# Column halves for the last row group, and row-by-row output stores in the last four blocks

## The chip, the cores and the metric

The kernel runs on one core of a Trainium2 chip. The metric is the device time of one execution in microseconds (us); a profiled execution also has a span, from the program's first recorded instruction to its last, about 1.8 us shorter. TensorE (the matmul engine) is called PE, its weight loads PEld, VectorE DVE, ScalarE ACT, GpSimd POOL and SyncE SP in the profile; a q after the name (SPq) marks work of the engine's sequencer, such as issuing a DMA.

## The reference, cut to what matters

```python
sig = 1.0 / (1.0 + np.exp(-f_logit))
f = lower_bound + (1.0 - lower_bound) * sig
for t in range(S):                       # recurrence over 6144 steps, 4 sequences
    h = f[:, t] * h + (1.0 - f[:, t]) * x[:, t]
    y[:, t] = h
y = y.reshape(24576, 256)
out = np.maximum(y @ w1, y @ w2) @ w_out # 256 -> 1024 -> 256, float32 out
```

## The kernel before

The 24576 tokens are worked in 48 blocks of 512 (`NBLK = 48`). For each block PE computes eight hidden tiles (`hidden`), ACT applies a relu, and PE projects the *previous* block's hidden tiles to the output. Output row `i` of a block (`i` = 0 to 3; 128 tokens) is ten accumulating matmuls of 256 columns: eight over hidden chunks and two over a linear part. Two rows make a group `g`, which shares a PSUM buffer (the memory in which PE's sums land), is copied to SBUF (on-chip memory) by DVE and stored by a DMA from SP. In the last block the second group is handled row by row, to shorten what follows the last matmul:

```python
opool = ctx.enter_context(tc.tile_pool(name="opool", bufs=8))
lastpool = ctx.enter_context(tc.tile_pool(name="last", bufs=2))
ps_o = ctx.enter_context(tc.tile_pool(name="ps_o", bufs=3, space=PS))
# ... cut ...
def send_out(j, g):
    r0 = j * TB + 2 * g * P
    nc.sync.dma_start(
        out=out[r0 : r0 + 2 * P, :].rearrange("(p r) d -> p r d", r=2),
        in_=osbs[j, g][:],                       # 128 partitions x 2 KB
    )

def store_row(j, g, r):
    osb = lastpool.tile([P, D], FP32, name="row")
    nc.vector.tensor_copy(out=osb[:], in_=pos[j, g, r][:, 0, :])
    nc.sync.dma_start(out=..., in_=osb[:])       # 128 partitions x 1 KB
# ... cut ...
for j in range(3, NBLK + 1):
    for fc in range(FC):
        if j < NBLK:
            hidden(j, fc)
        project(j - 1, fc)                       # half of one row per fc
        if fc == 0 and j > 3:
            store(j - 2, 1)
        if fc == 4 and j < NBLK:
            store(j - 1, 0)
        if j == NBLK and fc in (3, 5, 7):
            if fc == 3:
                store(j - 1, 0)
            else:
                store_row(j - 1, 1, (fc - 5) // 2)
```

Of the kernel before, what the change touches and what calls it, by code (L numbers as in the profile page):

```python
# [8 lines left out]
FP32 = mybir.dt.float32  # L9
# [3 lines left out]
P = 128  # L13
# [3 lines left out]
def kernel(  # L17
# [13 lines left out]
    nc = tc.nc  # L31

    B, S, D = x.shape
    DFF = moe_w1.shape[1]
    assert D == 2 * P and DFF == 8 * P
    KC = D // P
    FC = DFF // P
    TB = 512
# [3 lines left out]
    NBLK = B * NBB  # L42
# [16 lines left out]
    ypool = ctx.enter_context(tc.tile_pool(name="ypool", bufs=4))  # L59
    rpool = ctx.enter_context(tc.tile_pool(name="rpool", bufs=3 * FC))  # L60
    opool = ctx.enter_context(tc.tile_pool(name="opool", bufs=8))
    lastpool = ctx.enter_context(tc.tile_pool(name="last", bufs=2))
    PS = bass.MemoryType.PSUM
    ps_d = ctx.enter_context(tc.tile_pool(name="ps_d", bufs=5, space=PS))
    ps_o = ctx.enter_context(tc.tile_pool(name="ps_o", bufs=3, space=PS))
# [14 lines left out]
    wob = wpool.tile([P, FC, D], BF16)  # L80
    w1T = wpool.tile([P, FC, D], BF16)
    w13 = wpool.tile([P, KC, D], BF16)


    ins, us, vs, uT, vT, ffs, ys = {}, {}, {}, {}, {}, {}, {}

    def alloc_in(j):
        fn = inpool.tile([P, NQ, D], FP32, name="fn")
        xn = inpool.tile([P, NQ, D], FP32, name="xn")
        ins[j] = (fn, xn)  # L90
        us[j] = natpool.tile([P, NQ, D], BF16, name="un")
        vs[j] = natpool.tile([P, NQ, D], BF16, name="vn")
        ffs[j] = nffpool.tile([P, KC, TB], BF16, name="nff")
        ys[j] = ypool.tile([P, KC, TB], BF16, name="y")
# [81 lines left out]
    def turn_dma(c):  # L176
        for s, name in enumerate(("fs", "xs")):
            t = ttpool.tile([P, KC, CB * TB], BF16, name=("fT", "xT")[s])
            turned[c, s] = t
            nc.sync.dma_start_transpose(out=t[:], in_=spare[c % NS, name][:])  # L180

    def cast_behind(c):

        if c + 1 < NCH:
            last = CB * TB - 1
            nc.gpsimd.tensor_copy(out=held[:], in_=turned[c, 0][:, KC - 1, last : last + 1])  # L186
            cast(c + 1)
# [5 lines left out]
    def gate(j):  # L193
        ffs[j] = midpool.tile([P, KC, TB], BF16, name="ff")
        ys[j] = ypool.tile([P, KC, TB], BF16, name="y")
        us[j] = midpool.tile([P, KC, TB], BF16, name="u")
        nc.scalar.activation(out=us[j][:], in_=part(j, 0), func=AF.Sigmoid, scale=-1.0)  # L197

    def drive(j):
        vs[j] = midpool.tile([P, KC, TB], BF16, name="v")  # L200
        nc.vector.tensor_tensor(out=vs[j][:], in0=us[j][:], in1=part(j, 1), op=ALU.mult)  # L201

    def forget_half(j, h, on_act=False):
        forget(ffs[j][:, h, :], us[j][:, h, :], h, on_act)

    def scan_half(j, h):
        scan(j, h, 0, TB, vs[j][:, h, :])
# [7 lines left out]
    rts = {}  # L215
# [18 lines left out]
    def relu(j, fc, on_dve=False):  # L234
        rt = rpool.tile([P, TB], BF16, name="rt")
        rts[j, fc] = rt
        if on_dve:
            nc.vector.tensor_relu(out=rt[:], in_=dts[j, fc][:])
        else:
            nc.scalar.activation(out=rt[:], in_=dts[j, fc][:], func=AF.Relu)  # L240

    def hidden_whole(j, fc):
        dts[j, fc] = ps_d.tile([P, TB], FP32, name="dT")
        for kc in range(KC):
            nc.tensor.matmul(  # L245
                dts[j, fc][:],
                lhsT=wd[:, kc, unit(fc)],
                rhs=ys[j][:, kc, :],
                start=(kc == 0),
                stop=(kc == KC - 1),  # L250
            )

    def hidden(j, fc):
        hidden_whole(j, fc)
        relu(j, fc)

    pos = {}
# [31 lines left out]
    def project_steps(j, i, lo, hi):  # L289
        g, r = divmod(i, 2)  # L290
        alone = j == NBLK - 1 and g == 1
        if lo == 0 and (r == 0 or alone):
            pos[j, g, r] = ps_o.tile([P, 2, D], FP32, name="psO")
        ps = pos[j, g, r if alone else 0][:, 0 if alone else r, :]
        for s in range(lo, hi):
            step(
                j,
                i,
                s,
                ps,  # L300
                s == 0 and (r == 0 or alone),
                s == FC + KC - 1 and (r == 1 or alone),
            )

    def project(j, slot):
        i, half_ = divmod(slot, 2)
        n = FC + KC
        project_steps(j, i, half_ * n // 2, (half_ + 1) * n // 2)

    osbs = {}  # L310

    def copy_out(j, g, on_act=False):
        osbs[j, g] = opool.tile([P, 2, D], FP32, name="osb")
        if on_act:
            nc.scalar.copy(out=osbs[j, g][:], in_=pos[j, g, 0][:])
        else:
            nc.vector.tensor_copy(out=osbs[j, g][:], in_=pos[j, g, 0][:])  # L317

    def send_out(j, g):
        r0 = j * TB + 2 * g * P  # L320
        nc.sync.dma_start(
            out=out[r0 : r0 + 2 * P, :].rearrange("(p r) d -> p r d", r=2),
            in_=osbs[j, g][:],
        )

    def store(j, g):
        copy_out(j, g)
        send_out(j, g)

    def store_row(j, g, r):  # L330
        osb = lastpool.tile([P, D], FP32, name="row")
        nc.vector.tensor_copy(out=osb[:], in_=pos[j, g, r][:, 0, :])  # L332
        r0 = j * TB + 2 * g * P
        nc.sync.dma_start(
            out=out[r0 : r0 + 2 * P, :].rearrange("(p r) d -> p r d", r=2)[:, r, :],
            in_=osb[:],
        )


    QF = DFF // 4  # L340
# [90 lines left out]
    def keep_warm(n):  # L431
        for _ in range(n):
            nc.tensor.matmul(  # L433
                idle[:].rearrange("p r d -> p (r d)"),
                lhsT=warm[:, 0:P],
                rhs=warm[:],
                start=True,
                stop=True,
            )
# [29 lines left out]
    def load_item(name):  # L469
        if name[:2] == "wo":  # L470
            wout_load(int(name[2]))
        elif name[0] == "w":
            w, src = ((w1n, moe_w1), (w2n, moe_w2))[int(name[1]) - 1]
            weight_load(int(name[2]), w, src)
        else:
            half = ("ab".index(name[2]),) if len(name) == 3 else ()
            load(int(name[1]), "fx".index(name[0]), *half)
# [3 lines left out]
    def send_pending():  # L481

        while outs and turned:
            send_out(*outs.pop(0))
# [66 lines left out]
    with tc.manual_schedule():  # L551
        for j in range(NP):
            alloc_in(j)
        nc.scalar.dma_start(out=lbr[:], in_=lower_bound.rearrange("(h p) -> h p", p=P))
        for name in LOADS.split():
            load_item(name)
        nc.vector.memset(warm[:], 0.0)  # L557
        make_identity(nc, ident[:])
        nc.vector.tensor_copy(out=ident_b[:], in_=ident[:])
        keep_warm(7)  # L560
        for item in PLAN.split():
            issue(item)
        assert not outs

        for j in range(3, NBLK + 1):
            for fc in range(FC):
                if j < NBLK:
                    hidden(j, fc)
                project(j - 1, fc)
                if fc == 0 and j > 3:  # L570
                    store(j - 2, 1)
                if fc == 4 and j < NBLK:
                    store(j - 1, 0)
                if j == NBLK and fc in (3, 5, 7):
                    if fc == 3:
                        store(j - 1, 0)
                    else:
                        store_row(j - 1, 1, (fc - 5) // 2)
                if (j, fc) in gate_of:
                    b = gate_of[j, fc]  # L580
                    gate(b)
                    drive(b)
                    for h in range(KC):
                        forget_half(b, h)
                        scan_half(b, h)
                if (j, fc) in turn_of:
                    turn_dma(turn_of[j, fc])
                    cast_behind(turn_of[j, fc])
# [30 lines left out]
```

## Time and profile before

| | before |
|---|---|
| time, median of the first three runs | 397.38 us (397.21 to 397.80) |
| span of the profiled run | 395.60 us |
| last row: first matmul starts / last ends | 391.26 / 392.51 us |
| last copy ends, last store issued | 392.97, 393.00 us |
| last completion, end of span | 394.69, 395.60 us |

The rows to read are those at the very end, because PE is busy for nearly all of the time before them. The prediction below shows them and says what each tells. I call the time from the start of the last row's first matmul to the end of the span the **end stretch**: 395.60 - 391.26 = 4.35 us.

### The profile page before, as it was taken

The page shows a single profiled execution, that of the slowest core. Times are in us where ns is not written, and L with a number is a line of the kernel's source. Part 1 is how long each engine was busy: PE and PEld are TensorE (multiplying, and loading weights), DVE is VectorE, ACT ScalarE, POOL GpSimd, SP SyncE. Part 2 cuts the span into 40 slices and gives each one's busy share as a digit, 9 for nine tenths or more (in the row PEclk, how much of TensorE's full clock was granted, in tenths as well). Part 3 has the DMA queues.
Part 4 walks back from the last instruction along what each step waited for, and adds up shares of the span by engine and source line. Part 5 has one row for each costly group of instructions (what it writes and reads, how often), then busy time and mean ns, then how long its engine had stood idle before and what let it go on. Part 6 is the DMA issues. An engine that isn't in the chain of part 4 may idle for free.

```text
span 395.6 us, 7146 instructions
## 1 busy us (share of the span) xinstructions
PE 387.6 (98%) x2793; PEld 275.0 (70%) x2840; DVE 251.2 (63%) x366; ACT 273.3 (69%) x451; POOL 39.2 (10%) x83
## 2 busy tenths in 40 slices
PE   8999999999999999999999999999999999999996
PEld 3796777676667777767677777666677777676775
DVE  4896965756755775576567656755775576567622
ACT  4787676677667666766676677667766766676661
POOL 2511011011101101001011011011011010100000
PEclk9999999999999999999999999999999999999999
DMA  7989999999999999999999999999898898981122
GB/s 252 350 220 211 211 206 216 216 221 225 200 228 201 203 230 178 229 220 202 199 232 209 188 228 191 195 208 230 198 204 213 186 202 193 217 188 55 53 81 107
DMA packets 125078, 79.12 MB, mean 200 GB/s; under 512 B 94194, under 2 KB 101620, under 8 KB 125044
## 3 DMA queue, kind: packets, MB, share of 16 engines
q1 hardware_dynamic: 113072, 55.59, 59.8%
q0 software_dynamic: 11968, 23.07, 35.7%
q8 instruction: 22, 0.36, 0.4%
q14 instruction: 12, 0.10, 0.1%
q10 hardware_dynamic: 4, 0.00, 0.0%
HBM read 53.48 MB, written 48.23 MB: 257 GB/s over the span
## 4 chain that ended last, share of the span: by engine, by line
PE 95%; DMA 1%; DVE 1%; issue 1%; SPq 1%; DVEq 0%
PE psO L268 53%; PE dT L245 39%; PE dT L225 2%; DMA xn<-in_x_dram 1%; PE dT L126 1%; SPq L100 0%; PE psO L413 0%; DVE vn L113 0%; SPq L344 0%; DVE y L149 0%; DVE wd L388 0%; DVE wdf L380 0%; DVE row L332 0%; PE dT L396 0%; DVEq L113 0%
## 5 line engine op out<-in xcount | busy, mean ns | idle before, releaser
L240 ACT ACTIVATE rt<-dT 128x512 bf16<-128x512 f32 x382 | 222.9, 596 | 104.4 <-PE dT L245 101.2
L268 PE MATMUL psO<-wob,rt 128*128 128x256 bf16 x1536 | 231.0, 273 | 0.2
L268 PEld LDWEIGHTS <-rt 128*128 128x128 bf16 x1536 | 150.0, 98 | 94.7 <-issue 0.2
L245 PE MATMUL dT<-y,wd 128*128 128x512 bf16 x690 | 208.8, 379 | 2.2
L149 DVE TENSOR_TENSOR_SCAN y<-ff,y,v 128x512 bf16<-128x512 bf16 x82 | 105.2, 1283 | 2.9
L317 DVE COPY osb<-psO 128x512 f32<-128x512 f32 x93 | 62.6, 678 | 65.6 <-PE psO L268 65.6
L245 PEld LDWEIGHTS <-wd 128*128 128x128 bf16 x736 | 72.0, 98 | 8.8
L268 PE MATMUL psO<-w,y 128*128 128x256 bf16 x384 | 72.4, 273 | 0.0
L201 DVE TENSOR_TENSOR v<-u,xT 128x1024 bf16<-128x1024 bf16 x44 | 30.4, 691 | 62.7 <-ACT u L197 50.8
L197 ACT ACTIVATE u<-fT 128x1024 bf16<-128x1024 bf16 x44 | 46.1, 1049 | 3.1 <-DMA fT<-fs 3.1
L268 PEld LDWEIGHTS <-y 128*128 128x128 bf16 x384 | 37.6, 98 | 4.4
L186 POOL CAST held<-fT 128x1 f32<-128x1 bf16 x21 | 6.7, 319 | 278.9 <-DMA fT<-fs 278.9
L138 DVE TENSOR_SCALAR ff<-u,nom 128x512 bf16<-128x512 bf16 x88 | 29.7, 338 | 0.0
L170 POOL DMA_DIRECT2D fs<-in_f_logit_dram x22 | 12.3, 558 | 4.3 <-issue 4.3
L170 POOL DMA_DIRECT2D xs<-in_x_dram x22 | 12.1, 549 | 0.0
L149 DVE TENSOR_TENSOR_SCAN y<-nff,y,dT 128x256 bf16<-128x256 bf16 x14 | 9.6, 731 | 1.8 <-PE dT L126 1.5
L225 PE MATMUL dT<-y,wd 128*128 128x256 bf16 x64 | 10.1, 273 | 0.3 <-DVE wd L388 0.2
L433 PE MATMUL psO<-warm 128*128 128x512 bf16 x22 | 7.8, 492 | 1.2 <-DVE warm L557 1.2
L149 DVE TENSOR_TENSOR_SCAN y<-ff,v 128x512 bf16<-128x512 bf16 x6 | 7.4, 1225 | 0.2
L108 ACT ACTIVATE un<-fn 128x512 bf16<-128x512 f32 x8 | 5.0, 628 | 3.3 <-DMA fn<-in_f_logit_dram 3.0
L225 PEld LDWEIGHTS <-wd 128*128 128x128 bf16 x64 | 5.8, 98 | 1.4 <-issue 0.4
L113 DVE TENSOR_TENSOR vn<-un,xn 128x512 bf16<-128x512 bf16 x8 | 6.1, 767 | 1.0 <-DMA xn<-in_x_dram 1.0
(40 smaller groups left out, 52.2 us busy)
## 6 DMA issues: line engine op xcount, KB each, us to landing
out_dram<-osb SPq DMA_DIRECT2D x95, 256.0 KB, 3.4
fs<-in_f_logit_dram POOLq DMA_DIRECT2D x22, 512.0 KB, 6.8
xs<-in_x_dram POOLq DMA_DIRECT2D x22, 512.0 KB, 9.6
fn<-in_f_logit_dram SPq DMA_DIRECT2D x6, 256.0 KB, 6.0
xn<-in_x_dram SPq DMA_DIRECT2D x6, 256.0 KB, 5.7
w1n<-in_moe_w_dram SPq DMA_DIRECT2D x4, 256.0 KB, 5.9
w2n<-in_moe_w_dram SPq DMA_DIRECT2D x4, 256.0 KB, 6.0
won<-in_moe_w_out_dram SPq DMA_DIRECT2D x4, 256.0 KB, 6.0
```

The costliest lines, as they stand in the source:

```text
L138: nc.vector.tensor_scalar(out=o, in0=i, scalar1=nom[:, h : h + 1], scalar2=1.0, op0=ALU.mult, op1=ALU.add)
L149: nc.vector.tensor_tensor_scan(out=ys[j][:, h, t0:t1], data0=ffs[j][:, h, t0:t1], data1=v, initial=initial, op0=ALU.mult, op1=ALU.add,)
L170: nc.gpsimd.dma_start(out=spare[c % NS, name][:], in_=src[b, k * TB : (k + CB) * TB, :], max_dma_last_dim=4096,)
L186: nc.gpsimd.tensor_copy(out=held[:], in_=turned[c, 0][:, KC - 1, last : last + 1])
L197: nc.scalar.activation(out=us[j][:], in_=part(j, 0), func=AF.Sigmoid, scale=-1.0)
L201: nc.vector.tensor_tensor(out=vs[j][:], in0=us[j][:], in1=part(j, 1), op=ALU.mult)
L225: nc.tensor.matmul(dts[j, fc][:, tok], lhsT=wd[:, kc, unit(fc)], rhs=ys[j][:, kc, tok], start=(first and kc == 0), stop=(not first and kc ...
L240: nc.scalar.activation(out=rt[:], in_=dts[j, fc][:], func=AF.Relu)
L245: nc.tensor.matmul(dts[j, fc][:], lhsT=wd[:, kc, unit(fc)], rhs=ys[j][:, kc, :], start=(kc == 0), stop=(kc == KC - 1),)
L268: nc.tensor.matmul(ps, lhsT=lhsT, rhs=rhs, start=start, stop=stop, skip_group_check=True)
L317: nc.vector.tensor_copy(out=osbs[j, g][:], in_=pos[j, g, 0][:])
L433: nc.tensor.matmul(idle[:].rearrange("p r d -> p (r d)"), lhsT=warm[:, 0:P], rhs=warm[:], start=True, stop=True,)
```

## The change

The change wants the last piece of work to be small: the last row's left 128 columns are computed, copied and stored while PE computes the right 128, so that only half a row is left to copy and store at the end. And the stores of the last four blocks are split into two of 128 KB.

```diff
-    lastpool = ctx.enter_context(tc.tile_pool(name="last", bufs=2))
+    lastpool = ctx.enter_context(tc.tile_pool(name="last", bufs=3))
     def send_out(j, g):
-        nc.sync.dma_start(out=..., in_=osbs[j, g][:])
+        if j < NBLK - 4:
+            nc.sync.dma_start(out=rows_out(j, g), in_=osbs[j, g][:])
+            return
+        for r in range(2):
+            nc.sync.dma_start(out=rows_out(j, g)[:, r, :], in_=osbs[j, g][:, r, :])
+    def project_last(c):
+        cols = slice(c * P, (c + 1) * P)
+        ps = ps_o.tile([P, 2, D], FP32, name="psO")
+        for s in range(FC + KC):
+            ...  # lhsT as before; rhs is wob[:, s, cols] or w13[:, s - FC, cols]
+            nc.tensor.matmul(ps[:, 0, 0:P], lhsT=lhsT, rhs=rhs,
+                             start=(s == 0), stop=(s == FC + KC - 1))
+        store_last(1, c * P, (c + 1) * P, ps[:, 0, 0:P])   # copy and store this half
 # in the loop
+                if j == NBLK and fc > 5:
+                    project_last(fc - 6)
+                    continue
```

Seven groups are split: both of blocks 44 to 46 and the first of block 47. With the last row's second store that makes eight more SP stores than before.

More of the change, by code (lines that the diff above doesn't have):

```diff
@@ L317, in copy_out, with rows_out @@
             nc.vector.tensor_copy(out=osbs[j, g][:], in_=pos[j, g, 0][:])
+    def rows_out(j, g):
+        r0 = j * TB + 2 * g * P
+        return out[r0 : r0 + 2 * P, :].rearrange("(p r) d -> p r d", r=2)
     def send_out(j, g):
-        r0 = j * TB + 2 * g * P
-        nc.sync.dma_start(
-            out=out[r0 : r0 + 2 * P, :].rearrange("(p r) d -> p r d", r=2),
-            in_=osbs[j, g][:],
-        )
+        if j < NBLK - 4:
[3 more added lines that the diff above has]
+            nc.sync.dma_start(out=rows_out(j, g)[:, r, :], in_=osbs[j, g][:, r, :])
     def store(j, g):
@@ L328, in store, with store_last @@
         send_out(j, g)
-    def store_row(j, g, r):
+    def store_last(r, c0, c1, ps):
         osb = lastpool.tile([P, D], FP32, name="row")
-        nc.vector.tensor_copy(out=osb[:], in_=pos[j, g, r][:, 0, :])
-        r0 = j * TB + 2 * g * P
-        nc.sync.dma_start(
-            out=out[r0 : r0 + 2 * P, :].rearrange("(p r) d -> p r d", r=2)[:, r, :],
-            in_=osb[:],
-        )
+        nc.vector.tensor_copy(out=osb[:, c0:c1], in_=ps)
+        nc.sync.dma_start(out=rows_out(NBLK - 1, 1)[:, r, c0:c1], in_=osb[:, c0:c1])
+    def project_last(c):
+        cols = slice(c * P, (c + 1) * P)
+        ps = ps_o.tile([P, 2, D], FP32, name="psO")
+        tok = slice(2 * P + 1, 4 * P, 2)
+        j = NBLK - 1
+        for s in range(FC + KC):
+            if s < FC:
+                lhsT, rhs = rts[j, s][:, tok], wob[:, s, cols]
+            else:
+                lhsT, rhs = ys[j][:, s - FC, tok], w13[:, s - FC, cols]
+            nc.tensor.matmul(
+                ps[:, 0, 0:P], lhsT=lhsT, rhs=rhs, start=(s == 0), stop=(s == FC + KC - 1)
+            )
+        store_last(1, c * P, (c + 1) * P, ps[:, 0, 0:P])
     QF = DFF // 4
@@ L573 @@
                     store(j - 1, 0)
-                if j == NBLK and fc in (3, 5, 7):
-                    if fc == 3:
-                        store(j - 1, 0)
-                    else:
-                        store_row(j - 1, 1, (fc - 5) // 2)
+                if j == NBLK and fc == 3:
+                    store(j - 1, 0)
+                if j == NBLK and fc == 5:
+                    store_last(0, 0, D, pos[j - 1, 1, 0][:, 0, :])
                 if (j, fc) in gate_of:
```

## The prediction

> **What bounds the kernel now.** I read the head of the page first, then the chain that ended last in its last five microseconds, then the timeline and the busy times by stretch of the same window, and last the only 128-column matmuls that the kernel already has.
>
> ```profile
> span 395.6 us, 7146 instructions
> ...
> PE 387.6 (98%) x2793; PEld 275.0 (70%) x2840; DVE 251.2 (63%) x366; ACT 273.3 (69%) x451; POOL 39.2 (10%) x83
> ...
> PE 95%; DMA 1%; DVE 1%; issue 1%; SPq 1%; DVEq 0%
> ```
>
> TensorE (PE) is busy for 98% of the span and carries 95% of the chain. No other engine is near it. So a change that leaves the number of streamed matmul columns as it was, as this one does, can only win where PE is *not* working: in the opening, which the diff doesn't touch, and after the last matmul. The second is this (the chain in order of time, then the timeline from 391.1 us on, cut):
>
> ```profile
> 390.98 1.54 PE psO L268 x14
> 392.52 0.02 issue
> 392.55 0.42 DVE row L332
> ```
>
> ```profile
> 391.08 0.33 SPq L321 DMA_DIRECT2D out_dram<-osb  x1
> ...
> 391.26 1.04 PE L268 MATMUL psO<-wob,rt 128*128 128x256 bf16 x8
> 391.46 0.42 DVE L332 COPY row<-psO 128x256 f32<-128x256 f32 x1 [0.40 <-PE psO L268]
> 391.91 1.42 SPq L334 DMA_DIRECT2D out_dram<-row  x2
> ...
> 392.13 0.38 PE L268 MATMUL psO<-w,y 128*128 128x256 bf16 x2
> 392.55 0.42 DVE L332 COPY row<-psO 128x256 f32<-128x256 f32 x1 [0.67 <-PE psO L268]
> ```
>
> The last row group is ten matmuls of 256 columns, started from 391.26 to 392.24 us at a pitch of 0.109 us and done at 392.52. One DVE copy of 128x256 follows (0.42 us), ending at 392.97. The last store is issued at 393.00 (the two issues of the L334 line are 0.33 us each, the second ending at 391.91 + 1.42 = 393.33). Its data move like this (columns: stretch, its length, busy time of PE, PEld, DVE, ACT, POOL, clock, DMA share, GB/s):
>
> ```profile
> 391.90:392.75 0.85, 0.61 (x6) 0.30 (x4) 0.20 (x1) 0.00 (x0) 0.00 (x0) 1.00 0.85 308
> 392.75:393.28 0.53, 0.00 (x0) 0.00 (x0) 0.22 (x1) 0.00 (x0) 0.00 (x0) 1.00 0.74 247
> 393.28:393.82 0.54, 0.00 (x0) 0.00 (x0) 0.00 (x0) 0.00 (x0) 0.00 (x0) 1.00 0.00 0
> 393.82:394.36 0.54, 0.00 (x0) 0.00 (x0) 0.00 (x0) 0.00 (x0) 0.00 (x0) 1.00 0.73 243
> 394.36:395.60 1.24, 0.00 (x0) 0.00 (x0) 0.00 (x0) 0.00 (x0) 0.00 (x0) 0.86 0.02 7
> ```
>
> Three bursts: the 256 KB store of the group before, the 128 KB of the last but one row, a pause, and the 128 KB of the last row. So the end is a fixed ladder: issue at 393.00, first packet 0.82 us later, 0.53 us of data, then (from the semaphore records) the last completion at 394.69, 0.34 us after the last packet, then 0.91 us of closing barriers to 395.60. The whole tail after the last matmul is 3.1 us, 0.8% of the time. **That is the ceiling of the change**, and most of its rungs don't depend on size.
>
> **What the Trainium skill says.** First, "TensorE: Matmul & The Clock Gate", section "Back-to-back issue gap": an isolated warm 128-column matmul takes some 56 ns, but a sustained stream of weight load and matmul pairs about 81 ns at 128 columns. The trace has 128-column pairs only in bursts of four:
>
> ```profile
> 7.25 0.39 PE L126 MATMUL dT<-ident_b,un 128*128 128x128 bf16 x4
> 7.47 0.38 PE L433 MATMUL psO<-warm 128*128 128x512 bf16 x1
> ```
>
> Four matmuls from 7.25 to the next start at 7.47 are 0.22 / 4 = 0.056 us each, with a weight load apiece. So it agrees with the first figure; twenty in a row are not in this trace. Second, "DMA: Bandwidth & Descriptors", section "Anatomy of one DMA": most of a transfer's fixed cost is the wait for the write receipt, not data. The trace agrees: of the last store's 1.69 us from issue to completion only 0.53 us is data. Third, the same page, section "Queues, rings and completion order": on each DMA engine descriptors of one ring are consumed in order. All output stores are issued by SP, so a last store can stand behind those before it. In the kernel before it does not: the ring is empty from 393.28 to 393.82. Fourth, "Perfetto Trace Analysis", section "DMA Optimizations": splitting transfers lets parts start sooner when the engines are mostly idle. That is the intent here.
>
> **The change part by part.**
>
> *Matmuls of the last row.* Ten of 256 columns become ten of 128 for the left half and ten of 128 for the right, each with its own weight load (ten loads more). Before: 10 x 0.109 = 1.09 us. After, at 0.056 us: 20 x 0.056 = 1.12 us, all on the path. The last start moves from 392.24 to 391.26 + 19 x 0.056 = 392.32, but a 128-column record lasts 219 ns where a 256-column one lasts 272, so the end moves by 0.08 - 0.05 = **+0.02 us**. The right half needs a third PSUM buffer, the one emptied by the copy that ran from 390.37 to 391.06; it starts at about 391.82, so it doesn't wait.
>
> *The last copy.* 128x512 takes 0.692 us and 128x256 takes 0.425 us in this window: 1.04 ns per column. 128x128 should take 0.425 - 128 x 1.04 = 0.292 us. On the path: **-0.13 us**. The left half's copy (about 392.01 to 392.31) lies beside the right half's matmuls.
>
> *The last store.* 64 KB in 128 runs of 512 B instead of 128 KB in runs of 1 KB. Packet records: 87 ns for 2 KB, 48 ns for 1 KB, and 25 ns for the two 512 B packets in the trace (another queue). A burst of 1 KB packets, eight per engine, takes 0.52 us, that is 65 ns each, 17 over the record; with 26 + 17 = 43 ns the burst of 512 B packets takes 8 x 43 = 0.34 us: **-0.18 us**. First packet and receipt stay at 0.82 and 0.34 us.
>
> *The queue before it.* SP now issues the group before as two stores of 128 KB (391.09 and about 391.46; issue plus gap is 0.38 us), the first row (391.91), the left half (about 392.33) and the right half (about 392.89). SP is free each time just before the copy it waits for ends. But 1 KB packets carry less: 256 KB took 0.83 us in 2 KB packets and would take 2 x 0.52 = 1.04. From 391.91 the DMA engines then run without a pause: three bursts of 0.52 to 393.47, the left half to 393.81, and the right half, whose first packet could go at 392.89 + 0.82 = 393.71, waits **+0.10 us**.
>
> *Row by row in the four blocks.* Seven stores more; their 0.38 us of SP time each and 2 us to landing lie in stretches where DMA is at 0.2 of its capacity and SP issues one store in 2 to 6 us. No PE wait hangs on them (eight output buffers). **0.**
>
> Sum: +0.02 - 0.13 - 0.18 + 0.10 = **-0.19 us**; completion at 394.50 instead of 394.69, span about 395.4, time 397.38 - 0.19 = 397.2.
>
> **Rivals.**
>
> *A: the weight loads bind.* If twenty pairs in a row run at the 81 ns of the skill, the row takes 1.62 us, 0.53 more, and the kernel gets slower by 0.3 us: 397.7. At the 109 ns of today's pairs it would be +1.1 - 0.3 = +0.8 us: 398.2. Against both: 56 ns in bursts of four; a weight load record lasts 98 ns, but four loads are seen to start 56 ns apart. For it: no longer run is seen. I give it 15%.
>
> *B: no queue.* If engines overlap packets of neighbouring stores, the wait of 0.10 goes and the gain is 0.3 us: 397.1. If 512 B writes cost nearly what 1 KB writes do, the data term is zero and the queue grows by 0.18, so the change is about a wash: 397.4 to 397.6.
>
> *C: the fixed rungs hide it.* After its last issue SP steps through closing waits, in before from 393.38 to 394.23, until the last store's own completion ends it. With the issue 0.11 us earlier these would end near 394.1, still ahead of 394.5. So I don't expect it to bind.
>
> **Range and chances.** Every case above lies within 0.8 us, 0.2% of the time; two per cent would be 7.9 us, more than twice the whole tail. The three runs of before spread over 0.6 us, which is more than the expected effect, so the range is that spread around the expectation, a little wider above for rival A: 396.6 to 397.9. Chances: faster 0.005, same 0.99, slower 0.005.
>
> **What would show it.** Twenty 128-column matmuls at a pitch near 56 ns (rival A: 80 or more); a last copy of 128x128 near 0.29 us, ending about 0.11 us earlier than 392.97; the last issue near 392.89; DMA bursts without a pause from 391.9 to about 394.15; the closing barriers still 0.9 us. Everything before 355 us should be unchanged. The prediction is wrong if PE gains or loses anywhere else, if the right half waits for its PSUM buffer, or if the last completion comes later than 394.69.

## The result, and the profile after

The four runs of the changed kernel had a median of 397.37 us (396.94 to 397.76), the four of before 397.38. The ratio is 0.9998 with a 95% interval of 0.9981 to 1.0015. A ratio is the mean time of one kernel's runs over that of the other's of the same rounds, so it is not quite the ratio of the medians.

The head of the page and the shares of the chain:

```profile
span 395.4 us, 7223 instructions
...
PE 389.7 (99%) x2850; PEld 274.6 (69%) x2850; DVE 251.4 (64%) x367; ACT 273.4 (69%) x451; POOL 37.0 (9%) x83
...
PE 96%; DMA 1%; DVE 1%; SPq 1%; issue 0%; DVEq 0%
```

The bound is the same. The 2.1 us of additional PE busy time are most likely no work: the trace of before holds 2793 matmul records for 2840 weight loads, so some records are missing there; here there are 2850 of each.

The span is 0.2 us shorter, just what was predicted. That agreement is an accident. The last row starts at 390.77 us here and at 391.26 in before, 0.48 us earlier, and that lead is already there at 79 us, some 290 us before the first changed instruction. The same DVE copy in the timelines of before and after (the first two columns are start and length in us):

```profile
79.29 0.69 DVE L317 COPY osb<-psO 128x512 f32<-128x512 f32 x1 [2.12 <-PE psO L268]
```

```profile
78.81 0.69 DVE L317 COPY osb<-psO 128x512 f32<-128x512 f32 x1 [2.60 <-PE psO L268]
```

So the opening scatters from run to run, by more than the change is worth, and the end stretch must be read by itself. It is 395.42 - 390.77 = **4.64 us, 0.30 us longer than before**. The chain of the last microseconds, then the timeline (cut), then three lines from shorter windows that show the left half's copy, its store and the right half's store separately:

```profile
390.94 1.13 PE psO L350 x20
392.07 0.02 issue
392.09 0.29 DVE row L336
```

```profile
390.60 0.81 SPq L328 DMA_DIRECT2D out_dram<-osb  x2
...
390.77 0.61 PE L350 MATMUL psO<-wob,rt 128*128 128x128 bf16 x8
...
391.52 1.59 SPq L337 DMA_DIRECT2D out_dram<-row  x3
...
392.09 0.29 DVE L336 COPY row<-psO 128x128 f32<-128x128 f32 x1 [0.27 <-PE psO L350]
```

```profile
391.53 0.29 DVE L336 COPY row<-psO 128x128 f32<-128x128 f32 x1
```

```profile
392.30 0.34 SPq L337 DMA_DIRECT2D out_dram<-row  x1
```

```profile
392.75 0.37 SPq L337 DMA_DIRECT2D out_dram<-row  x1
```

The left half is copied by 391.82 but its store is issued only at 392.30. The right half is copied by 392.38 but its store is issued only at 392.75, because SP is still busy with the left one until 392.64. In the kernel before the last store follows its copy by 0.03 us; here it follows by 0.36. The data of the stores (columns as in the prediction):

```profile
391.42:392.93 1.51, 0.63 (x12) 0.46 (x9) 0.58 (x2) 0.00 (x0) 0.00 (x0) 1.00 0.80 261
392.93:393.12 0.19, 0.00 (x0) 0.00 (x0) 0.00 (x0) 0.00 (x0) 0.00 (x0) 1.00 0.19 43
393.12:393.45 0.33, 0.00 (x0) 0.00 (x0) 0.00 (x0) 0.00 (x0) 0.00 (x0) 1.00 0.65 185
393.45:393.60 0.15, 0.00 (x0) 0.00 (x0) 0.00 (x0) 0.00 (x0) 0.00 (x0) 1.00 0.06 17
393.60:393.95 0.35, 0.00 (x0) 0.00 (x0) 0.00 (x0) 0.00 (x0) 0.00 (x0) 1.00 0.65 186
```

There is no queue in front of the last two bursts: they stand alone, each 0.33 to 0.35 us long, with pauses before them. So the DMA engines waited for SP, not SP for them.

**What SP waited for.** Nothing that the program orders: its semaphores were up. SP's records in the trace, counted from zero in order of start, show this in both kernels (pause = time since the end of the record before; from the trace's records, not from a view):

```
before   334  wait        393.736
         335  wait        394.114   pause 0.350   (closing waits)
after    334  wait        391.948   (before the left half's store)
         335  DMA issue   392.302   pause 0.337
```

It is the same number, 335, in both. The same pause stands before records 79 and 207, that is, every 128 records (0.44 and 0.34 us in both kernels). And 0.6 to 1.1 us after each, one 8 KB packet appears on DMA queue 14, which the page lists as "instruction": at 394.74 us in before, at 392.94 in after. Counted from the end of record 334 it comes 0.97 to 1.27 us later in all thirteen traces, also where the pause itself is hidden in a wait. (The trace of before has nine more 8 KB packets on this queue at other times, so the link rests on the timing.) The Trainium skill, "Runtime: NRT & Kernel Launch", section "Instruction fetch mechanics", says that an engine refills its instruction memory in blocks through a DMA queue of its own, and calls the cost of crossing a block boundary mostly hidden. So the reading is: SP pauses a third of a microsecond at a block boundary of its own instructions. Before, the boundary fell in the closing waits, at a time when the last store was still under way, and cost nothing. The eight added stores moved it onto the left half's store.

### The profile page after: what moved, and what is told of

The parts are those of the page before. It is cut to its first block, busy times and chain, and to the rows that moved or that the text cites. A ratio compares the mean times of both kernels' runs of the same rounds, so it can differ in the third digit from the quotient of the medians.

```text
span 395.4 us, 7223 instructions
## 1 busy us (share of the span) xinstructions
PE 389.7 (99%) x2850; PEld 274.6 (69%) x2850; DVE 251.4 (64%) x367; ACT 273.4 (69%) x451; POOL 37.0 (9%) x83
## 4 chain that ended last, share of the span: by engine, by line
PE 96%; DMA 1%; DVE 1%; SPq 1%; issue 0%; DVEq 0%
PE psO L268 53%; PE dT L245 40%; PE dT L225 2%; DMA xn<-in_x_dram 1%; PE dT L126 1%; SPq L100 0%; PE psO L429 0%; DVE vn L113 0%; PE psO L350 0%; SPq L360 0%; DVE y L149 0%; DVE wd L404 0%; DVE wdf L396 0%; DVE row L336 0%; PE dT L412 0%
## 5 line engine op out<-in xcount | busy, mean ns | idle before, releaser
L245 PE MATMUL dT<-y,wd 128*128 128x512 bf16 x736 | 218.6, 379 | 0.0
L186 POOL CAST held<-fT 128x1 f32<-128x1 bf16 x21 | 4.0, 192 | 280.0 <-DMA fT<-fs 280.0
```

Source lines behind the costliest of these rows:

```text
L245: nc.tensor.matmul(dts[j, fc][:], lhsT=wd[:, kc, unit(fc)], rhs=ys[j][:, kc, :], start=(kc == 0), stop=(kc == KC - 1),)
```

## The experiments

My theory was that pause. The rival was that the row-by-row stores crowd SP or the DMA queue. A third, that the halves themselves are slow, was tested with them. Eleven runs were made, two of them of the unedited kernels and one a repeat; all gave correct results. The table has each one's end stretch in parts, all counted from the start of the last row's first matmul; completion is the last semaphore update of the last store.

| kernel | last store issued | last completion | completion to end | end stretch |
|---|---|---|---|---|
| before | 1.75 | 3.44 | 0.91 | 4.35 |
| before again | 1.75 | 3.44 | 0.92 | 4.35 |
| change | 1.97 | 3.74 | 0.91 | 4.64 |
| change again | 1.97 | 3.79 | 0.91 | 4.69 |
| rows alone | 1.75 | 3.66 | 0.97 | 4.63 |
| halves alone | 1.64 | 3.24 | 1.68 | 4.91 |
| change, eight blocks by rows | 1.73 | 3.35 | 0.91 | 4.26 |
| halves, seven groups by rows early | 1.83 | 3.50 | 0.91 | 4.41 |
| halves, three groups by rows early | 1.64 | 3.23 | 1.16 | 4.39 |
| halves, fifteen groups by rows early | 1.64 | 3.20 | 0.91 | 4.11 |
| the same again | 1.64 | 3.19 | 0.91 | 4.10 |
| change, right half stored from ACT | 1.64 | 3.64 | 0.91 | 4.56 |
| halves alone, whole last block by halves | 1.64 | 3.24 | 1.69 | 4.93 |

### How firm the measure is

The kernel before and the changed kernel were each run once more without an edit.

> The kernel before once more, to see how firm its last microseconds are. If the end stretch (start of the last row's first matmul to end of span) is set by the program, it is again 4.30 to 4.40 us (4.35 in the first profile) and the last completion comes 3.4 to 3.5 us after the row's start, whatever the whole time is. If it scatters by 0.2 us or more, differences of that size between the other runs mean nothing.

> The changed kernel once more, unaltered, to see how firm its last microseconds are. Measure: from the start of the first matmul of the last row to the end of the span (the end stretch): before 395.60 - 391.26 = 4.35 us, after 395.42 - 390.77 = 4.64 us. Theory (a pause of SyncE before its instruction number 335, which falls on the store of the left half): again 4.6 to 4.7 us, with a pause of 0.3 to 0.4 us between the wait before the left half's store and that store. Rival (chance of one run): the stretch scatters by 0.2 us or more. Whole time: 397.2 to 397.6 us, same as before within the noise.

Measured: 4.352 us (first 4.346), with the last row starting at 391.64 where the first profile has 391.26; and 4.694 (first 4.644). So the end stretch is firm to 0.05 us while the whole time scatters by several tenths. The second sample of the change was also slower as a whole: 398.04 us median, ratio 1.0021, interval 1.0005 to 1.0036. The eight runs of its two samples average 397.68 and the thirteen runs of before beside them 397.35; the difference of 0.33 agrees with the 0.30 to 0.34 of the end stretch, but with this scatter the profile carries the verdict, not the mean.

### Halves alone

```diff
-        if j < NBLK - 4:
+        if True:
```

> The column halves, but all earlier stores whole, as in the kernel before. SyncE then has seven instructions fewer before the last stores, so number 335 falls among the closing waits. Theory: the left half's store goes out 0.03 us after its copy, the right half's likewise (1.64 us after the row's first matmul), the stores in front take 0.83 + 0.52 + 0.33 us of the DMA engines and are done before the right half is ready; last completion 3.15 us after the row's start (3.44 in the kernel before), end stretch 4.05 us, 0.3 us better than before. Rival (the halves themselves cost it, by a slow 512-byte store or the issues of three stores in a row): end stretch 4.4 us or more. The whole time moves by less than its noise in either case: 397.0 to 397.5.

The issue (1.64) was as expected, and the completion (3.24) nearly so, 0.20 us earlier than before: the halves do what they were meant to. The end stretch of 4.91 fits neither side. What grew is the time from completion to end, 1.68 in place of 0.91. The waits of SP in the last ten microseconds say where:

```profile
SPq L632 <- DMA out_dram<-row: 1.2, 1, 1.2
```

In this kernel SP's wait for the last store lasts 1.2 us and, by SP's records, is the *second* of its nine closing waits. SP waits in the end for all DMA completion semaphores in a fixed order. Stores take eight of them in turn. Before and in the change, the last store has the eighth, so the other waits are passed while it is still under way. One store more than before, and the last store has the first; seven waits of 0.065 us then follow *behind* it, and among them the pause before record 335, 0.34 us where the gap is else 0.04: 0.91 + 7 x 0.065 + 0.30 = 1.67, measured 1.68. The whole time agrees in direction: 397.62 us, ratio 1.0013 (1.0001 to 1.0026).

### Three groups early: a dose of the closing list

```diff
-        if j < NBLK - 4:
+        if not (36, 0) <= (j, g) <= (37, 0):
```

> As the halves alone, with only three groups sent row by row, in block 36 and the first half of 37. The last store then has the fourth of the eight completion semaphores in place of the first, and SyncE's number 335 is the second of the closing waits, before the wait for the last store. Theory (closing list): the completion comes 3.2 to 3.3 us after the row's first matmul as in the halves alone, four more waits of 0.065 us follow it, and no pause: 0.91 + 0.26 = 1.17 us from completion to end (halves alone 1.68, before 0.91), end stretch 4.35 to 4.5 us. Rival (halves alone is slow at the end for some reason of the halves): 1.6 us or more again, 4.9 us.

Measured: 1.16 us from completion to end (expected 1.17), end stretch 4.39. The last store has the fourth semaphore, four waits follow it, and the pause lies before. The order of the closing list explains it; the halves do not.

### The pause without late row stores, and late row stores without the pause

Both edit the same line of the changed kernel. The first moves seven split groups to blocks 34 to 37, the second splits eight blocks in place of four:

```diff
-        if j < NBLK - 4:
+        if not (34, 0) <= (j, g) <= (37, 0):     # seven groups early
```

```diff
-        if j < NBLK - 4:
+        if j < NBLK - 8:                         # eight blocks
```

> Column halves, and seven groups sent row by row as in the change, but in blocks 34 to 37, some 80 us before the end. The last stores then follow whole stores as in the halves alone, but SyncE's instruction number 335 is again the store of the left half. Theory (the pause): the pause of 0.3 to 0.4 us is back before the left half's store though no row store is near; the right half's issue comes about 1.85 us after the row's first matmul in place of 1.64, end stretch 4.3 to 4.55 us. Rival (row stores in front crowd SyncE or the DMA queue): no pause, end stretch 4.05 us as with the halves alone.

> The change, but with the stores of the last eight blocks sent row by row in place of four: more of what the rival blames, and eight SyncE instructions more before the end, so that number 335 falls on the first row store of block 46's second half, which waits three microseconds anyway. Theory (the pause): no pause at the left half's store; the right half's goes out 1.65 to 1.70 us after the row's first matmul (1.97 in the change), end stretch 4.1 to 4.25 us. Rival (row stores crowd SyncE or the DMA queue): 4.6 us as in the change, or more.

With seven groups early, the left half's copy and store (two windows of one timeline):

```profile
392.42 0.29 DVE L336 COPY row<-psO 128x128 f32<-128x128 f32 x1
```

```profile
393.04 0.34 SPq L337 DMA_DIRECT2D out_dram<-row  x1
```

The copy ends at 392.71 and the store goes out at 393.04: a pause of 0.34 us before SP's record 335, with no split group within 75 us. With eight blocks by rows:

```profile
391.21 0.29 DVE L336 COPY row<-psO 128x128 f32<-128x128 f32 x1
```

```profile
391.68 0.40 SPq L337 DMA_DIRECT2D out_dram<-row  x1
```

The copy ends at 391.50 and the left half's store starts at 391.68, with SP busy by the row store before it until 391.59; there is no pause, although there are more row stores. Record 335 is now a store of block 46, before which SP idles for three microseconds anyway. So the pause follows the instruction number, and the rival's crowding is not its cause. The crowding is real but smaller: the eight-block kernel needs 4.26 us, 0.15 more than the same halves behind whole stores (4.11). In these last microseconds an issue lasts 0.33 us alone and 0.37 to 0.43 us directly behind another. The last store goes out 0.09 us later than behind whole stores; the other 0.06 us lie between its issue and its completion.

### Rows alone

The edit of `send_out` alone, on the kernel before.

> The other half of the change alone: stores of the last four blocks row by row, the last row computed and stored whole as in the kernel before. SyncE's number 335 is then the store of the last row, and the pause of 0.35 us falls while SyncE waits for that row's copy anyway (from about 1.2 to 1.7 us after the row's first matmul). Theory: the last store goes out at 1.75 us as in the kernel before, completion at 3.45 to 3.55 us (an instruction fetch of 8 KB may hold one DMA engine up), one wait more in the closing list, end stretch 4.4 to 4.5 us (before 4.35, change 4.64). Rival (row stores crowd the end): the last store is issued late or completes after 3.7 us, 4.6 us or more.

The last store went out at 1.75 us as expected, the pause being hidden. The rest is a miss: completion at 3.66 and 4.63 us in all, an end stretch in the rival's band. Of the 0.28 us over before, 0.07 is the one wait more in the closing list, as expected, and 0.22 lies between issue and completion. Landing times of the two row stores, of before and of this kernel:

```profile
DMA to landing us min/median/max: 1.7/1.7/1.7
```

```profile
DMA to landing us min/median/max: 1.8/1.8/1.9
```

Of the last store's sixteen completion updates fifteen were in by 3.44 us, as in before, and a single one came at 3.66. The 8 KB instruction packet ran on one DMA engine from 2.17 to 2.70 us, just ahead of the last store's data (first packets at 2.57). Among these data one 1 KB packet, started at 2.79, took 253 ns where the others took some 48, and the packet of the last update started at 3.25, 0.17 us after the one before it. I read the straggler as that engine's share; the records don't name the engine. Crowding by row stores would hardly spare fifteen of sixteen.

### Right half stored from ACT

```diff
-        nc.sync.dma_start(out=rows_out(NBLK - 1, 1)[:, r, c0:c1], in_=osb[:, c0:c1])
+        eng = nc.scalar if c0 else nc.sync
+        eng.dma_start(out=rows_out(NBLK - 1, 1)[:, r, c0:c1], in_=osb[:, c0:c1])
```

> The change, with the store of the right half issued by ScalarE, which is idle by then, not by SyncE. Theory (SyncE's pause delays the two last stores; the DMA engines have room): SyncE's pause and the late store of the left half stay (1.53 us after the row's first matmul), but the right half's store goes out at about 1.64 us in place of 1.97; completion at 3.3 to 3.5 us in place of 3.74, end stretch 4.2 to 4.4 us in place of 4.64. Rival (the DMA engines or the descriptor queue are what is full): issue earlier, but completion still at 3.7 us, end stretch 4.6 us.

```profile
392.66 0.29 DVE L336 COPY row<-psO 128x128 f32<-128x128 f32 x1 [0.27 <-PE psO L351]
392.87 0.34 SPq L338 DMA_DIRECT2D out_dram<-row  x1
392.98 0.38 ACTq L338 DMA_DIRECT2D out_dram<-row  x1
```

ACT issues the right half 0.03 us after its copy while SP is still at the left half, so SP was what held it. But the completion, 3.64 us, is only 0.10 earlier than in the change, against an expectation of 3.3 to 3.5: again one of the store's sixteen updates came last, 0.27 us after the other fifteen, with the instruction packet on an engine from 2.16 to 2.74 us. So the earlier issue gained little here. In the two kernels with the boundary far from the end (eight blocks; fifteen groups) the last store's sixteen updates lie within 0.20 us with no straggler. Over all thirteen traces, one update comes 0.22 to 0.45 us behind the other fifteen in exactly the five where the packet ran between 2.0 and 3.0 us: on the left half's store in the change (both samples), with seven groups early and here, and on the last store in rows alone. The right half straggles too, by 0.14 and 0.18 us in the change and by 0.27 here, but only by 0.04 with seven groups early. In the other eight traces the last store's last update is at most 0.03 us behind. So the packet goes with the straggler wherever it falls on the last stores; it was not isolated as the cause, since the packet comes with the boundary.

### Does a longer run of 128-column matmuls slow down?

The halves alone, with all four rows of the last block by halves: 80 pairs in place of 20.

```diff
     def project(j, slot):
         i, half_ = divmod(slot, 2)
+        if j == NBLK - 1:
+            project_narrow(j, i, half_)   # ten matmuls of 128 columns
+            return
```

> As the halves alone, but all four rows of the last block are computed by column halves: 80 pairs of weight load and 128-column matmul in a row in place of 20. If a pair costs 0.056 us however long the run of pairs is, the last matmul starts 79 x 0.056 = 4.4 us after the first of them. If [...]the sustained 81 ns of the Trainium skill takes over, later pairs are 0.08 us apart and the run takes 5 to 6.4 us. The end after the last matmul should be as in the halves alone (closing list behind the last store), end stretch some 4.9 us.

```profile
388.00 0.61 PE L319 MATMUL psO<-wob,rt 128*128 128x128 bf16 x8
...
392.35 0.28 PE L376 MATMUL psO<-w,y 128*128 128x128 bf16 x2
```

The first of 80 starts at 388.00, the last one 4.41 us later (79 x 0.056 = 4.42). No spacing among the 80 records is over 0.056 us. For runs of up to 80 pairs, four times what the change needs, rival A of the prediction has nothing left.

### A version that avoids both

```diff
-        if j < NBLK - 4:
+        if not (30, 0) <= (j, g) <= (37, 0):
```

Fifteen groups are sent by rows, long before the end: sixteen more stores than before, so the last store keeps the eighth semaphore, and record 335 is a store six microseconds before the last row.

> Column halves, the last blocks' stores whole, and fifteen groups sent row by row in blocks 30 to 37. That adds sixteen output stores to the kernel before, a multiple of the eight completion semaphores that SyncE's DMAs take in turn, so the last store has again the semaphore that the closing list waits for last; and it puts SyncE's instruction number 335 on the store of block 46's first half, some six microseconds before the last row starts, where SyncE waits anyway. Theory (pause and closing list, not the halves, made the two earlier kernels slow): the right half's store goes out about 1.64 us after the row's first matmul, its completion comes 3.2 us after it (3.24 in the halves alone), 0.91 us of closing follow, end stretch 4.1 to 4.2 us (before 4.35, change 4.64, halves alone 4.91). Rival (three stores in a row at the end cost it): 4.4 us or more. Whole time 0.2 us below that of before, inside its noise: 397.0 to 397.4.

> The kernel with fifteen groups sent row by row early, unaltered, once more, to see whether its end stretch holds (4.05 to 4.2 us; 4.11 in its first profile) and whether five more rounds can tell its whole time from that of before. Expected gain 0.24 us of 397; with single runs scattering by some 0.4 us, the interval of the ratio will most likely hold 1.

```profile
391.90 0.29 DVE L336 COPY row<-psO 128x128 f32<-128x128 f32 x1 [0.27 <-PE psO L350]
```

```profile
392.22 0.34 SPq L337 DMA_DIRECT2D out_dram<-row  x1
```

The store follows the copy by 0.03 us and the end stretch is 4.11 and 4.10 us: 0.24 shorter than before, 0.53 to 0.59 shorter than the change. Whole times: 397.31 us (ratio 1.0001, 0.9987 to 1.0014) and 397.17 us (ratio 0.9990, 0.9977 to 1.0004). Its ten runs average 397.11 and the eighteen of before beside them 397.35, a difference of 0.24 us, as the profile has it; both intervals hold 1, so the time alone does not show it.

## Why the prediction was right or wrong

The range and the chances held for the first sample, and the ground for them did: all of it happens in a tail of three to four microseconds, of which 2% of the time would be twice as much. The sign of the small expected gain was wrong, and the first sample's 397.37 hid that by its faster opening; the second sample, 398.04, lies outside the range. The prediction's own sign of being wrong, a last completion later than 394.69 us, did not show for the same reason: it came at 394.51, but counted from the start of the last row at 3.74 in place of 3.44. By its steps, against the change's first profile:

- **Matmuls of the last row, +0.02 us.** Right: 1.280 us from first start to last end in place of 1.255. The chance of 15% given to binding weight loads was too high, as the 80 pairs show.
- **The last copy, -0.13 us.** Right: 0.292 us in place of 0.425.
- **The PSUM buffer of the right half doesn't wait.** Right: its first matmul follows the left half's last at 0.056 us.
- **"SP is free each time just before the copy it waits for ends."** This is the step that failed. I counted SP's issues at 0.33 us each and its gaps at 0.05, as the trace of before shows them, and did not ask where SP's own block boundary would fall after eight more stores. The pause, visible in the trace of before at record 335 in the closing waits, moved onto the left half's store, which kept SP busy until after the right half's copy had ended. From copy to issue 0.36 us passed in place of 0.03: **+0.33 us** for an expected zero.
- **The last store's data and the queue, -0.18 + 0.10 = -0.08 us.** From issue to completion 1.77 us in place of 1.69, **+0.07**. The data term was right (bursts of 0.33 to 0.35 us, expected 0.34; the working puts in 26 ns for a packet that it had read as 25, which changes nothing). The queue did not form in the change since its stores came late; in its place one completion straggled. Where no pause disturbs (eight blocks) issue to completion is 1.625 us, -0.07 (predicted -0.08).
- **Closing, 0.** Right for the change, 0.91 us. Rival C's case, the closing waits binding, did not occur in the change, but did in the halves alone.
- **Row by row in the four blocks, 0.** Wrong in an indirect way: they cost no engine anything, yet their number decides where SP's boundary falls and which semaphore the last store gets.

Sum: +0.02 - 0.13 + 0.33 + 0.07 = +0.30 us (rounded terms give 0.29), as measured. The same ledger for the eight-block kernel, where the pause is taken away (and eight more groups are split), reads +0.02 - 0.13 + 0.09 - 0.07 = -0.09: measured 4.26 - 4.35 = -0.09. So the prediction's mechanism was right where nothing paused, a gain of half the predicted size, since the issues, directly behind one another, cost 0.09 us that I had not counted.

That the pause follows SP's record number is shown; that it is a fetch of instructions is read from the packets' timing and the skill. What stays open: how much of the straggler is the instruction packet's own doing, and what SP does during the pause, since the packet that follows it comes 0.6 us later and so isn't what it waits for.

## What to carry to other kernels

When what is left to gain is some tenths of a microsecond behind the last matmul, count the instructions of the issuing queue as well as their durations: look in the trace for a pause that recurs at a fixed count, and see where the count falls after the edit. Look also at which of the closing waits is for the last transfer, since whatever stands behind it in the list is added to the end. Judge such a change by a stretch of the profile that starts after the noise, not by the whole time.

## What the Trainium skill lacked or had wrong

- "Runtime: NRT & Kernel Launch", "Instruction fetch mechanics": it gives refill blocks of 16 KiB (256 instructions) and calls a crossing mostly hidden. In all thirteen traces SyncE's boundaries are 128 records apart (79, 207, 335), with 8 KB packets on queue 14 (queue 8 does carry 16 KB packets, 22 in before; whether the block size was set otherwise for SyncE isn't known here); the pause there is 0.34 us wherever it isn't covered by a wait (0.44 at record 79), and 0.3 us of it came onto the path.
- "TensorE: Matmul & The Clock Gate", "Back-to-back issue gap": it gives some 81 ns per pair for a sustained stream of weight loads and 128-column matmuls. Here 80 pairs in a row ran at 56 ns.
- "DMA: Bandwidth & Descriptors", "Specifications": it gives 512 B as the least transfer for line rate. Stores to HBM with no other transfer beside them moved 308 GB/s in runs of 2 KB, 243 to 247 in runs of 1 KB and 185 in runs of 512 B (bursts of 256, 128 and 64 KB, so that start and end of a burst weigh more in the later figures).
- No page has these as durations: a DMA issue on SyncE lasts 0.33 us alone and 0.37 to 0.43 us directly behind another in the last microseconds; and the closing waits for DMA semaphores run in a fixed order at 0.065 us each, so a last store with the first of eight semaphores ends the program 7 x 0.065 = 0.45 us later than one with the last (an estimate; 1.68 in place of 0.91 us were measured, with 0.30 of the pause in it).
